# Low parts on another engine, an earlier normalisation and spread token parts in an attention kernel with two gated layers

## Chip, cores and metric

The kernel runs on one core of one Trainium2 chip. The time is the device time of one execution in microseconds, given as the median of three runs. Profile numbers come from one profiled execution, in us from its first instruction.

## What is computed

Pooled attention, then a gated layer, then a layer with a rational function, all in float32.

```python
k_p = k.reshape(B, H, Sp, pool, D).mean(axis=3)      # B, H = 8, 8; pool = 8; Sp = 72; D = 64
v_p = v.reshape(B, H, Sp, pool, D).mean(axis=3)
scores = scale * np.matmul(q, k_p.transpose(0, 1, 3, 2))
attn = softmax(scores)                               # maximum subtracted, sum + 1e-9
x = np.matmul(attn, v_p)                             # as 4608 tokens x 512
x = (silu(x @ w_gate) * (x @ w_val)) @ w_out         # 512 -> 1536 -> 512
h = x @ w_in                                         # 512 -> 2048
P = a[0] + a[1]*h + a[2]*h**2 + a[3]*h**3
Q = 1 + abs(b[0])*abs(h) + abs(b[1])*h**2
out = (P / (Q + 1e-6)) @ w_out2
```

## The kernel before

The 4608 tokens are nine blocks of 512. Every operand of a large product is held as two parts, a high one that TensorE takes at its fast float32 rate and a low one, the rest (`split`: ScalarE copies the high part, another engine subtracts). A product is then three matmuls per piece, high by high, low weights by high, high by low (`mm3`): the low part of the moving operand is wanted only in the last third.

The program writes the order of every engine by hand: each engine, and each queue of transfers (SP's, ScalarE's), carries out its instructions in the order of the program. `plan` holds the attention's steps by slot (one slot is one pass of f) and place; `place(stage, f, p)` runs what is due. The places of a pass are, in order, 0, A, B, B2 and C.

*Attention* works on units of up to 128 tokens. `scores` issues the score products; its four closures are `soft1` (VectorE: maximum per head, subtraction), `soft_exp` (ScalarE), `soft2` (VectorE: sum, 1e-9, reciprocal; then the product of probabilities and reciprocal, on GpSimd where `early` or `helped`) and `soft3` (copies `pr`). `transposes` turns the result on TensorE into PSUM banks of the pool that also holds the scores. In `attention_slots` a unit's `soft1` stands at place 0 of the slot after its scores, its exponential at A, its `soft2` at B2, and its `soft3` and transposes at 0 and A of the next slot.

*Start and block 0.* The first block's four units run by themselves (L509 to L578), with steps of `first` between them. `first` (class `Weights`) brings the first layer's weights from 64-bit words to float32 and into two parts, in a pipeline of four: ScalarE prepares the words (`words`), VectorE bounds, shifts and selects (L120, L121, L114) and GpSimd adds (L117), ScalarE copies the high part (L165), and `step` subtracts the low part (L149) on VectorE or on the engine that it is given. Block 0's loop (L754 on, j = 0) makes three steps in each of its 12 passes of f, two of them with GpSimd for the low part. A pass has three products: gate (`gp`), value (`vp`) and, one pass late, output (`acc`). L783 multiplies the silu by the value product, L788 makes its low part.

*Blocks 1 and 2* run the same loop, with sums of the weights (`weight_sums`) for what follows.

*The pairs' stage* (L878 to L952) takes six blocks as three pairs by a scheme of seven products for eight: 36 passes n, 12 for each pair. In a pass TensorE's chain is s1 (`cc`), s2 (`ca`), then the closing a22 of the pass before, a12 (`cb`), s4 (`cc`), the opening a11 of the next pass (`ca`, and ScalarE copies it to `cb`), and s3 (`ca`). Each uses its own part of the pair's tokens: t1, t2, t4, b21, b22, b11, t3. `token_part` splits one of them: two copies by ScalarE, two subtractions by VectorE (L94). Between the products VectorE sums banks: L901 after s2 (its result is the bank that s4 goes on with) and L937 after s3 (which must have read the bank before a22 goes on). While pair p runs, the next pair's attention runs in the same passes, the second layer's weights are converted (`second`: L120, L121, L114 by VectorE, L117 and the low part L94 by GpSimd), and in passes 2 to 9 the output weights' sums: `out_sums` (VectorE L651, then GpSimd L655 to L658) in one pass, `out_parts` (ScalarE, VectorE L94) in the next. Weights are streamed from memory two passes ahead (`stream`).

After it come the pairs' output products and the second layer, which the change leaves alone.

Of the kernel before, what the change touches and what calls it, by code (L numbers as in the profile page):

```python
# [13 lines left out]
AF = mybir.ActivationFunctionType  # L14
# [49 lines left out]
def attention_gated_rational(  # L64
# [277 lines left out]
    def scores(u, qt, early=False, helped=False):  # L342
# [25 lines left out]
        def soft1():  # L368
            for half in range(2):
                sc = banks[half]  # L370
                nc.vector.tensor_reduce(mx[:n, half], sc[:n], axis=AX.X, op=ALU.max)
                nc.vector.tensor_tensor(
                    pt[:n, half::2], sc[:n],
                    mx[:n, half].unsqueeze(2).to_broadcast([n, 4, SP]), op=ALU.subtract,
                )

        def soft_exp():
            nc.scalar.activation(pt[:n], pt[:n], AF.Exp, scale=1.0 / (POOL * math.sqrt(D)))

        def soft2():  # L380
            nc.vector.tensor_reduce(sm[:n], pt[:n], axis=AX.X, op=ALU.add)
            nc.vector.tensor_scalar(sm[:n], sm[:n], 1e-9, None, op0=ALU.add)
            nc.vector.reciprocal(sm[:n], sm[:n])
            (nc.gpsimd if early or helped else nc.vector).tensor_tensor(  # L384
                pt[:n], pt[:n], sm[:n].unsqueeze(2).to_broadcast([n, H, SP]), op=ALU.mult
            )

        def soft3():
            pairs = pt.rearrange("p (a i) s -> p a (i s)", i=2)
            for c in range(2):  # L390
                src = pairs[:n, 2 * c : 2 * c + 2, P:].unsqueeze(1).to_broadcast([n, 3, 2, REST])
                if early:
                    nc.scalar.activation(pr[:n, c], src, AF.Copy)
                else:
                    nc.gpsimd.tensor_copy(pr[:n, c], src)
# [69 lines left out]
    def attention_slots(js, start, helped=False):  # L465
# [16 lines left out]
        for n, (g, i) in enumerate(fl):  # L482
# [3 lines left out]
            put(slot, "C", lambda u=u: box.__setitem__(("s", u), scores(u, box.pop(("q", u)), helped=helped)))  # L486
            put(slot + 1, "0", lambda u=u: box["s", u][0]())
            put(slot + 1, "A", lambda u=u: box["s", u][1]())
            put(slot + 1, "B2", lambda u=u: box["s", u][2]())
# [24 lines left out]
    qts = {flat0[0]: qload(flat0[0], True, nc.scalar)}  # L514
    nc.scalar.dma_start(ident, ident_in)
# [3 lines left out]
    for u in flat0[1:]:  # L519
        qts[u] = qload(u, True, nc.scalar)  # L520
# [17 lines left out]
    soft = [scores(u, qts[u], True) for u in flat0]  # L538
# [14 lines left out]
    for n in range(2):  # L553
        soft[n][0]()
        soft[n][1]()
# [11 lines left out]
    for n in range(last):  # L567
        if n + 1 < last:
            turn(n + 1)
        for fn in evacs[n]:  # L570
            fn()
        if n:
            lows[n - 1]()
        lows[n] = values([flat0[n]], ptTs[n], None, x)
        if n + 1 < last:
            first.step(6)
# [165 lines left out]
    for j in range(PLAIN):  # L742
# [11 lines left out]
        for f in range(NF1):  # L754
# [20 lines left out]
            if j == 0:  # L775
                first.step(6, nc.gpsimd)
# [9 lines left out]
            if j == 0:  # L786
                first.step(6, nc.gpsimd)
# [92 lines left out]
    for key in ("t2", "b21", "b22", "t3", "t4"):  # L880
        token_part(0, key)
    stream(1)
    for n in range(full_n):
# [17 lines left out]
        nc.vector.tensor_tensor(c, cq[n][:, 0, :], bank_a[n], op=ALU.add)  # L901
        place(stage, f, "A")
        if n:
            end_chain(n - 1)
        if f == 0 and p:
            token_part(p, "t4")
# [9 lines left out]
        if more:  # L916
            token_part(p + 1, "b21")
# [4 lines left out]
        if more:  # L922
            token_part(p + 1, "b22")
# [13 lines left out]
        nc.vector.tensor_tensor(cq[n][:, 1, :], cq[n][:, 0, :], bank_a[n], op=ALU.add)  # L937
        if more:
            token_part(p + 1, "t3")
# [279 lines left out]
```

## Time and profile before

| | |
|---|---|
| Time, median of 3 runs | 1858.56 us (1857.02 to 1859.35) |
| Profiled execution, whole | 1855.71 us |
| Its span | 1853.9 us |
| TensorE busy | 1773.1 us, 96% of the span |
| VectorE busy | 1404.3 us, 76% |
| ScalarE busy | 1133.9 us, 61% |
| GpSimd busy | 365.4 us, 20% |

Engines: PE is TensorE, DVE VectorE, ACT ScalarE, POOL GpSimd. A matmul's record counts pipelined time, so a busy PE isn't PE at its peak; its idle time is real. The shares of the span are means over stages with different limits: block 0 runs from 41 to 168 us, blocks 1 and 2 to 425, the pairs' stage to about 870 (its third pair, without attention, from about 750 on), the rest after it. Spans on POOL are rough.

### The profile page before, as it was taken

The page shows a single profiled execution, that of the slowest core. Times are in us where ns is not written, and L with a number is a line of the kernel's source. Part 1 is how long each engine was busy: PE and PEld are TensorE (multiplying, and loading weights), DVE is VectorE, ACT ScalarE, POOL GpSimd, SP SyncE. Part 2 cuts the span into 40 slices and gives each one's busy share as a digit, 9 for nine tenths or more (in the row PEclk, how much of TensorE's full clock was granted, in tenths as well). Part 3 has the DMA queues.
Part 4 walks back from the last instruction along what each step waited for, and adds up shares of the span by engine and source line. Part 5 has one row for each costly group of instructions (what it writes and reads, how often), then busy time and mean ns, then how long its engine had stood idle before and what let it go on. Part 6 is the DMA issues. An engine that isn't in the chain of part 4 may idle for free.

```text
span 1853.9 us, 23836 instructions
## 1 busy us (share of the span) xinstructions
PE 1773.1 (96%) x8212; PEld 1428.0 (77%) x8212; DVE 1404.3 (76%) x2315; ACT 1133.9 (61%) x1972; POOL 365.4 (20%) x506
## 2 busy tenths in 40 slices
PE   5889999998999999999999999999999999999998
PEld 5667877776777777787888788888888888888887
DVE  8997665547667665644777798888888989888987
ACT  5676455546665664434455667676677677667665
POOL 2665555442344335221000000000000000000000
PEclk9999999999999999999999999999999999999999
DMA  7531757559999987999935801010101010101000
GB/s 257 192 109 48 237 166 237 193 185 320 326 336 309 309 313 260 301 341 380 337 148 193 284 1 46 1 46 1 46 1 46 1 46 1 46 1 46 1 24 23
DMA packets 157464, 285.27 MB, mean 154 GB/s; under 512 B 12320, under 2 KB 78496, under 8 KB 156320
## 3 DMA queue, kind: packets, MB, share of 16 engines
q1 hardware_dynamic: 156192, 282.64, 44.1%
q8 instruction: 65, 1.06, 0.2%
q10 hardware_dynamic: 1152, 1.12, 0.2%
q14 instruction: 55, 0.45, 0.1%
HBM read 194.58 MB, written 89.13 MB: 153 GB/s over the span
## 4 chain that ended last, share of the span: by engine, by line
PE 77%; DVE 11%; POOL 4%; ACT 3%; issue 3%; DMA 2%; SPq 0%; POOLq 0%; DVEq 0%; ACTq 0%
PE acco L256 21%; PE h L256 21%; PE ca L256 7%; PE ya L1062 5%; PE vp L256 4%; PE cc L256 3%; PE acc L256 3%; PE gp L256 3%; PE yc L1062 3%; PE cb L256 2%; PE pv L440 1%; PE yb L1062 1%; POOL p L384 1%; PE sc L363 1%; DVE tg L121 1%
## 5 line engine op out<-in xcount | busy, mean ns | idle before, releaser
L256 PE MATMUL acco<-wo,gt 128*128 128x512 f32 x1728 | 426.5, 395 | 2.7 <-ACT gt L1149 2.2
L256 PE MATMUL h<-z,wi 128*128 128x512 f32 x1728 | 422.4, 393 | 0.0
L256 PEld LDWEIGHTS acco<-wo,gt 128*128 128x128 f32 x1728 | 324.9, 188 | 80.9 <-ACT gt L1149 3.1
L256 PEld LDWEIGHTS h<-z,wi 128*128 128x128 f32 x1728 | 324.3, 188 | 75.6
L1128 ACT ACTIVATE sq<-h 128x512 f32<-128x512 f32 x144 | 86.4, 600 | 221.2 <-PE h L256 221.2
L1135 DVE SCALAR_TENSOR_TENSOR w<-sq,neg,w 128x512 f32<-128x512 f32 x144 | 108.0, 750 | 67.4 <-ACT w L1129 62.7
L256 PE MATMUL gp<-x,wg 128*128 128x512 f32 x432 | 109.6, 400 | 9.1 <-POOL wg L149 9.1
L1145 DVE SCALAR_TENSOR_TENSOR g<-t,neg,e 128x512 f32<-128x512 f32 x144 | 108.2, 751 | 5.1
L1132 ACT ACTIVATE t<-h,neg 128x512 f32<-128x512 f32 x144 | 111.8, 777 | 0.0
L1141 DVE SCALAR_TENSOR_TENSOR t<-t,neg,h 128x512 f32<-128x512 f32 x144 | 107.7, 748 | 5.1
L256 PE MATMUL vp<-x,wv 128*128 128x512 f32 x432 | 110.6, 403 | 0.4
L1142 DVE SCALAR_TENSOR_TENSOR e<-w,ln 128x512 f32<-128x512 f32 x144 | 98.7, 686 | 13.5 <-ACT ln L1139 13.4
L1139 ACT ACTIVATE ln<-ln,lnb 128x512 f32<-128x512 f32 x144 | 104.2, 724 | 4.7
L256 PE MATMUL acc<-ht,wo 128*128 128x512 f32 x432 | 106.5, 396 | 0.0
L1143 DVE SCALAR_TENSOR_TENSOR e<-e,ln 128x512 f32<-128x512 f32 x144 | 99.7, 692 | 5.0
L256 PEld LDWEIGHTS gp<-x,wg 128*128 128x128 f32 x432 | 79.4, 188 | 29.9 <-POOL wg L149 11.7
L1149 ACT ACTIVATE gt<-g 128x512 fp32r<-128x512 f32 x144 | 90.7, 630 | 16.9 <-DVE g L1145 16.9
L1129 ACT ACTIVATE w<-h,cab 128x512 f32<-128x512 f32 x144 | 98.5, 684 | 2.6 <-DVE e L1142 2.6
L1150 DVE TENSOR_TENSOR gt<-g,gt 128x512 fp32r<-128x512 f32 x144 | 98.6, 685 | 1.5 <-ACT gt L1149 0.8
L1140 DVE TENSOR_TENSOR t<-t,h 128x512 f32<-128x512 f32 x144 | 98.0, 680 | 0.0
L256 PEld LDWEIGHTS vp<-x,wv 128*128 128x128 f32 x432 | 80.7, 191 | 20.3 <-POOL wv L149 2.6
L256 PEld LDWEIGHTS acc<-ht,wo 128*128 128x128 f32 x432 | 80.4, 188 | 18.2
(246 smaller groups left out, 3186.4 us busy)
## 6 DMA issues: line engine op xcount, KB each, us to landing
sw<-sd SPq DMA_DIRECT2D x72, 512.0 KB, 7.2
sw<-wd SPq DMA_DIRECT2D x36, 512.0 KB, 5.8
h<-hq SPq DMA_DIRECT2D x36, 512.0 KB, 5.9
sd<-sp SPq DMA_DIRECT2D x24, 512.0 KB, 4.0
sw<-vd SPq DMA_DIRECT2D x36, 256.0 KB, 7.5
hl<-h SPq DMA_DIRECT2D x18, 512.0 KB, 7.2
hr<-h SPq DMA_DIRECT2D x18, 512.0 KB, 9.7
out<-ob SPq DMA_DIRECT2D x36, 256.0 KB, 4.1
```

Source lines behind the costliest of these rows:

```text
L256: nc.tensor.matmul(acc, st[:, lw, cols], mv[:, rw, mcols], start=first and i == 0, stop=last and i == n - 1, skip_group_check=seeded,)
L1062: nc.tensor.matmul(banks[q], w[:, lw, cols], t[:, rw, :], start=opened and k == 0 and m == 0, stop=k == NK - 1 and m == 2, skip_group_chec ...
L1129: nc.scalar.activation(w0, hps, AF.Abs, scale=cab[:, 4:5])
L1132: nc.scalar.activation(t, hps, AF.Identity, scale=neg[:, 3:4], bias=neg[:, 2:3])
L1135: nc.vector.scalar_tensor_tensor(w0, sq, neg[:, 5:6], w0, op0=ALU.mult, op1=ALU.add)
L1139: nc.scalar.activation(ln, ln, AF.Exp, scale=-1.0, bias=lnb)
L1140: nc.vector.tensor_tensor(t, t, hps, op=ALU.mult)
L1141: nc.vector.scalar_tensor_tensor(t, t, neg[:, 1:2], hps, op0=ALU.add, op1=ALU.mult)
L1142: nc.vector.scalar_tensor_tensor(e, w0, C1, ln, op0=ALU.add, op1=ALU.mult)
L1143: nc.vector.scalar_tensor_tensor(e, e, 2.0, ln, op0=ALU.subtract, op1=ALU.mult)
L1145: nc.vector.scalar_tensor_tensor(g, t, neg[:, 0:1], e, op0=ALU.add, op1=ALU.mult)
L1150: lambda gt=gt, g=g: nc.vector.tensor_tensor(gt[:, 1, :], g, f32(gt[:, 0, :]), op=ALU.subtract),
```

## The change

Six edits.

1. In block 0, the low parts that GpSimd made (`first.step(6, nc.gpsimd)`, two in a pass) are made by VectorE. The addition at L117 stays on GpSimd.
2. At the start, units 0 and 1 take a new form of the softmax (`heads`): no subtraction; VectorE scales the negative maximum, and ScalarE runs eight Exp per unit straight from the banks, each with the maximum as bias and its sum as accumulator. Both units' `soft1` and exponentials stand ahead of the v reductions.
3. q of unit 1 is loaded by SP's queue ahead of v, q of units 2 and 3 by SP's queue behind v, where all three went by ScalarE's.
4. The copies `pr` of block 0 are made by GpSimd, no longer by ScalarE, and one step of `first` (at n = 0 of the four turns) is left out, so that every later step comes one place later.
5. For the pairs' attention `soft2` stands at B, not B2; these slots begin in block 2.
6. Token parts: pair 0 splits only `t1` and `t2` ahead of its first pass; `b21` and `b22` follow L901 of that pass, `t3` the silu of `cc`, `t4` L937. For the later pairs `b11`, `t1`, `t2` stay in the last pass of the pair before, `b21` moves behind its L937, and `b22`, `t3`, `t4` into the first pass of their own pair.

```diff
-    def scores(u, qt, early=False, helped=False):
+    SCALE = 1.0 / (POOL * math.sqrt(D))
+    def scores(u, qt, early=False, helped=False, heads=False):
...
                 nc.vector.tensor_reduce(mx[:n, half], sc[:n], axis=AX.X, op=ALU.max)
+                if heads:
+                    continue
...
+            if heads:
+                nc.vector.tensor_scalar(mx[:n], mx[:n], -SCALE, None, op0=ALU.mult)
...
         def soft_exp():
-            nc.scalar.activation(pt[:n], pt[:n], AF.Exp, scale=1.0 / (POOL * math.sqrt(D)))
+            if not heads:
+                nc.scalar.activation(pt[:n], pt[:n], AF.Exp, scale=SCALE)
+                return
+            for half in range(2):
+                for c in range(NPAIR):
+                    h = 2 * c + half
+                    nc.scalar.activation(
+                        pt[:n, h], banks[half][:n, c], AF.Exp, scale=SCALE, bias=mx[:n, half, c : c + 1],
+                        accum_out=sm[:n, h : h + 1],
+                    )
...
-            nc.vector.tensor_reduce(sm[:n], pt[:n], axis=AX.X, op=ALU.add)
+            if not heads:
+                nc.vector.tensor_reduce(sm[:n], pt[:n], axis=AX.X, op=ALU.add)
...
-                if early:
-                    nc.scalar.activation(pr[:n, c], src, AF.Copy)
-                else:
-                    nc.gpsimd.tensor_copy(pr[:n, c], src)
+                nc.gpsimd.tensor_copy(pr[:n, c], src)
...
-            put(slot + 1, "B2", lambda u=u: box["s", u][2]())
+            put(slot + 1, "B" if js[0] >= PLAIN else "B2", lambda u=u: box["s", u][2]())
...
+    qts[flat0[1]] = qload(flat0[1], True)
...
-    for u in flat0[1:]:
-        qts[u] = qload(u, True, nc.scalar)
+    for u in flat0[2:]:
+        qts[u] = qload(u, True)
...
-    soft = [scores(u, qts[u], True) for u in flat0]
+    soft = [scores(u, qts[u], True, heads=n < 2) for n, u in enumerate(flat0)]
+    for n in range(2):
+        soft[n][0]()
+        soft[n][1]()
     for r in vruns:
         r()
...
-    for n in range(2):
-        soft[n][0]()
-        soft[n][1]()
...
-        if n + 1 < last:
+        if 0 < n < last - 1:
             first.step(6)
...
             if j == 0:
-                first.step(6, nc.gpsimd)
+                first.step(6)
...
     begin_chain(0)
-    for key in ("t2", "b21", "b22", "t3", "t4"):
-        token_part(0, key)
+    token_part(0, "t2")
...
         nc.vector.tensor_tensor(c, cq[n][:, 0, :], bank_a[n], op=ALU.add)
+        if f == 0:
+            if n == 0:
+                token_part(p, "b21")
+            token_part(p, "b22")
         place(stage, f, "A")
         if n:
             end_chain(n - 1)
-        if f == 0 and p:
-            token_part(p, "t4")
...
-        if more:
-            token_part(p + 1, "b21")
         run()
...
         nc.scalar.activation(hq[n][:, 1, :], c, AF.Silu)
-        if more:
-            token_part(p + 1, "b22")
+        if f == 0:
+            token_part(p, "t3")
...
         nc.vector.tensor_tensor(cq[n][:, 1, :], cq[n][:, 0, :], bank_a[n], op=ALU.add)
+        if f == 0:
+            token_part(p, "t4")
         if more:
-            token_part(p + 1, "t3")
+            token_part(p + 1, "b21")
```

## Rows read from the trace of the kernel before

**Rows 1.** Busy us (x instructions) by engine, PEclk, DMA share, GB/s, by stretch.
```profile
41.00:168.00 127.00, 109.16 (x521) 82.94 (x519) 122.38 (x182) 90.41 (x146) 79.45 (x69) 0.97 0.35 119
...
425.00:755.00 330.00, 301.84 (x1553) 241.71 (x1554) 220.43 (x433) 204.37 (x376) 125.22 (x175) 0.97 0.90 309
```
**Rows 2.** TensorE's waits, 425 to 755 us: total us, times, longest.
```profile
PE t L412 <- POOL p L384: 12.9, 8, 3.3
PE cc L256 <- DVE cc L901: 6.3, 3, 5.1
PE ca L256 <- DVE cq L937: 5.1, 2, 2.9
PE t L412 <- POOL pr L395: 2.5, 4, 0.6
PE t L416 <- DVE p L372: 1.3, 4, 0.4
```
**Rows 3.** Pieces in time at the start, VectorE: start, us, line, out<-in.
```profile
14.21 0.46 DVE L372 TENSOR_TENSOR p<-sc,mx 128x288 f32<-128x288 f32 x1
```
**Rows 4.** Groups by line, VectorE, 41 to 168 us: busy us, mean ns | idle.
```profile
L114 DVE SCALAR_TENSOR_TENSOR rawo<-rawo,to 128x512 uint32<-128x512 uint32 x11 | 14.5, 1316 | 0.4
L121 DVE TENSOR_SCALAR tg<-tg 128x512 uint32<-128x512 uint32 x10 | 13.9, 1392 | 0.3
L121 DVE TENSOR_SCALAR to<-to 128x512 uint32<-128x512 uint32 x11 | 13.7, 1247 | 0.4
...
L149 DVE TENSOR_TENSOR wo<-rawo,wo 128x512 fp32r<-128x512 f32 x9 | 6.2, 689 | 0.0
...
L121 DVE TENSOR_SCALAR tv<-tv 128x512 uint32<-128x512 uint32 x11 | 4.7, 427 | 0.4
```
**Rows 5.** Pieces in time in block 0, GpSimd and VectorE.
```profile
78.45 1.04 POOL L117 TENSOR_TENSOR rawo<-rawo 128x512 uint32<-128x512 uint32 x1 [0.63 <-DVE rawo L114]
79.45 1.51 POOL L149 TENSOR_TENSOR wv<-rawv,wv 128x512 fp32r<-128x512 f32 x1
...
78.89 0.89 DVE L120 TENSOR_SCALAR tg<-tg 128x512 f32<-128x512 f32 x1
79.81 1.43 DVE L121 TENSOR_SCALAR tg<-tg 128x512 uint32<-128x512 uint32 x1
```
**Rows 6.** Groups by line, GpSimd, 41 to 168 us.
```profile
L149 POOL TENSOR_TENSOR wg<-rawg,wg 128x512 fp32r<-128x512 f32 x9 | 13.4, 1485 | 0.0
```
**Rows 7.** Pieces at 460 us: ScalarE's exponential, VectorE's sum.
```profile
463.40 0.69 ACT L378 ACTIVATE p<-p 64x576 f32<-64x576 f32 x1
...
464.80 0.74 DVE L381 TENSOR_REDUCE sm<-p 64x8 f32<-64x576 f32 x1
```
**Rows 8.** Pieces at 488 us, GpSimd and TensorE.
```profile
488.22 0.72 POOL L658 TENSOR_TENSOR os<-or,os 128x256 f32<-128x256 f32 x1
488.90 1.15 POOL L384 TENSOR_TENSOR p<-p,sm 128x576 f32<-128x576 f32 x1
...
490.10 0.66 PE L412 MATMUL t<-ident,p 128*128 128x128 f32 x4 [3.30 <-POOL p L384]
```
**Rows 9.** Two short stretches, columns as in rows 1.
```profile
490.00:500.00 10.00, 9.90 (x48) 7.95 (x48) 3.82 (x8) 7.15 (x10) 1.86 (x5) 0.83 0.97 333
...
646.00:656.00 10.00, 10.00 (x44) 8.40 (x45) 2.50 (x6) 6.41 (x11) 3.34 (x6) 0.83 0.98 344
```
**Rows 10.** TensorE's waits, 300 to 425 us (block 2).
```profile
PE t L412 <- POOL p L384: 1.3, 1, 1.3
```
**Rows 11.** Pieces where pairs 0 and 1 begin, VectorE and TensorE.
```profile
434.31 2.49 DVE L94 TENSOR_TENSOR x0t<-t,x0t 128x512 fp32r<-128x512 f32 x4
...
443.86 1.52 PE L256 MATMUL ca<-x0t,sw 128*128 128x512 f32 x6
...
603.70 0.74 DVE L381 TENSOR_REDUCE sm<-p 128x8 f32<-128x576 f32 x1
...
602.91 1.52 PE L256 MATMUL ca<-x1t,sw 128*128 128x512 f32 x6
```

More of the change, by code (lines that the diff above doesn't have):

```diff
@@ L463, in attention_gated_rational, with attention_slots @@
     plan = {}
-    def attention_slots(js, start, helped=False):
+    def attention_slots(js, start, helped=False, heads=False):
         def put(slot, place, fn):
@@ L485, in attention_slots @@
             put(slot - 1, "B2", lambda u=u: box.__setitem__(("q", u), qload(u)))
-            put(slot, "C", lambda u=u: box.__setitem__(("s", u), scores(u, box.pop(("q", u)), helped=helped)))
+            put(slot, "C", lambda u=u: box.__setitem__(("s", u), scores(u, box.pop(("q", u)), False, helped, heads)))
             put(slot + 1, "0", lambda u=u: box["s", u][0]())
-            put(slot + 1, "A", lambda u=u: box["s", u][1]())
-            put(slot + 1, "B2", lambda u=u: box["s", u][2]())
+            put(slot + 1, "0" if heads else "A", lambda u=u: box["s", u][1]())
+            put(slot + 1, "B" if js[0] >= PLAIN else "B2", lambda u=u: box["s", u][2]())
             put(slot + 2, "0", lambda u=u: box.pop(("s", u))[3]())
@@ L786, in attention_gated_rational @@
             if j == 0:
-                first.step(6, nc.gpsimd)
+                first.step(6)
             nc.vector.tensor_tensor(ht[:, 1, :], hh, f32(ht[:, 0, :]), op=ALU.subtract)
```

## The prediction, made before the changed kernel was run

> **What bounds the kernel now.** I read the busy times by stage first [rows 1]. In block 0 (41 to 168 us) VectorE is busy for 122.4 of 127 us and TensorE for 109.2: VectorE sets the pace there. In the pairs' stage (425 to 755 us) VectorE is busy for only 220 of 330 us, and TensorE leaves 28 us empty, so single waits set the end. Before 41 us TensorE waits for the first units' softmax, on which VectorE works from 14 us on [rows 3]. Next I read what TensorE waits for in the pairs' stage [rows 2]: 12.9 us in eight waits for GpSimd's normalisation (`p`, L384), 2.5 us for its copies (`pr`), 1.3 us for VectorE to free a score bank (`p`, L372), 6.3 us for the sum at L901 (5.1 of it once), 5.1 us for the sum at L937 in two waits. Last I read durations in block 0 [rows 4] and the two engines beside each other [rows 5].
>
> **Low parts of block 0 by VectorE.** Twenty-two subtractions leave GpSimd, where one takes 1.49 us [rows 6]. On VectorE the same line takes 0.69 us, with 0.6 from start to start [rows 4]: plus 13.2 us on the engine that sets the pace. Against it stands blocked time. The same tensor_scalar takes 0.43 us on one tile and 1.39 on another, and the selection on `rawo` takes 1.32 us where that on `rawv` takes 0.69 [rows 4]. The pieces show why: VectorE's 0.43 us operation begun at 79.81 ends only after GpSimd's low part that began at 79.45, and the operation at 78.89 lasts until after GpSimd's addition that began at 78.45 [rows 5]. Three groups alone lose 10 x 0.96 + 11 x 0.82 + 11 x 0.63 = 25.6 us. About 1.98 us per pass of f stand beside a low part, 21.8 us in eleven passes, and that part goes. The additions at L117 (1.04 us, three per pass) stay, and now find the moved low parts, which read two tiles, right behind them. I lay a pass out by starts: selection of `g`, low part first, the addition waits, then blocks the next operation for 0.9 us; the second addition runs beside the product with a bank (0.6 us not blocked) and holds the next low part for 0.5; the third lies behind the reductions. That is 1.4 us per pass where about 0.95 stand now (0.47 at 78.89 [rows 5], the rest on `to`). Sum: 13.2 - 21.8 + 11 x 0.45 = -3.6, and I take **-4.0** since GpSimd also starts its additions sooner. Bounds: -12 if the three groups' loss goes whole, +14 if none goes.
>
> The Trainium skill speaks on both sides here. "SBUF — State Buffer", section Who interferes with whom, says that a VectorE instruction with two SBUF inputs, or in a two-port mode, and a GpSimd instruction that reads SBUF exclude each other for a whole instruction, and the pieces agree: 1.43 us instead of 0.43 [rows 5]. By it alone, with every remaining addition blocking VectorE for its full 1.04 us, 33 x 1.04 in place of 11 x 0.95, this term would be about 13.2 - 21.8 + 23.9 = +15.3, near rival (1).
>
> **The start.** For units 0 and 1 four subtractions of 0.46 us go [rows 3] and two sums of 0.74 us [rows 7]; two scalings of about 0.2 come; one step of the weights (a bound, a shift and a selection, 1.5 us, and a low part of 0.6) moves to the end of the block. On VectorE this is -1.84 - 1.48 + 0.4 - 2.1 = -5.0. The maxima move ahead of the v reductions into time in which VectorE waits for loads (+1.6 back), but the missing step also covered TensorE's first values, so VectorE then waits some 1.8 us for them: **-4.8**. Sixteen short Exp with an accumulator take the place of two, and none is in this trace: at the most each takes as long as the whole one, 0.69 us [rows 7], 11 us together, of which about 3 would show; at the least they show nowhere. ScalarE is idle there, so I take none; bounds for the start -7 and +1. The q loads change from ScalarE's queue to SP's, unit 1's ahead of v, the others behind it; v then lands by one load later at most, which I count in the 1.8. The copies `pr` by GpSimd in place of ScalarE I take at nothing: GpSimd waits there for the reciprocals. The displaced step returns at f = 10 and 11, where the last steps were empty: **+1.3** (bounds 0 and 2.1).
>
> **Normalisation at B instead of B2.** Around 488 us the chain is plain: GpSimd ends its four sums of the output weights (the last at 488.22), only then runs `p` at 488.90 for 1.15 us, and TensorE's transposes start at 490.10 after 3.30 us of idling [rows 8]. At B the same work stands in front of those sums, of GpSimd's low parts and, on VectorE, of the additions at L651. By program order three more products and the next unit's scores (about 5 us) then lie between, so 12.9 + 2.5 should go. What is late next is the score bank: the transposes use banks that the next unit's subtraction frees, and behind the low part of the output weights VectorE is still busy with it; I leave 2 us of such waits. **-13.4**. The granted clock is 0.83 over 490 to 500 us [rows 9], 1.7 us lost to the lower of its two levels (1.2 GHz) after the 3.3 us gap, and it is 0.83 again over 646 to 656 us, behind another of the eight waits: **-3.4** for the two. In block 2, where the same line changes, one such wait of 1.3 us stands [rows 10], with 0.5 of bank waits: **-1.8**; there the product of the gate comes 1.1 us later behind the sum, and the output product that needs it runs a whole pass later, which covers it. Bounds for these three together: -8 and -21.
>
> VectorE now meets the sum at B, so what stands behind it waits if the exponential isn't done: the output weights' additions, then L937 and, through it, the last product of the chain. In a pass at 460 us the exponential ends at 464.09 and VectorE asks for it at 464.80 [rows 7], so I count nothing.
>
> **Token parts between the products.** They issue nothing on SP's queue; on ScalarE their high halves now stand ahead of one exponential per pair, and pair 0's second stream is asked for ahead of them. In pair 0 eight of the ten halves leave VectorE's queue in front of L901, where four of them take 2.49 us [rows 11]. By the new order: scores' maxima and subtractions to 433.7, L901 to 434.3, `b21` to 435.5, `b22` to 436.7, the conversion and the softmax sum to 438.8; ScalarE's silu tables and both silu hold `t3`'s high half until 440, so its low half ends at 440.9 and the product s3 at 441.3. It ended at 443.86 + 1.52 = 445.4 [rows 11]: **-4.1** (bounds -5 and -2). In pair 1 VectorE's queue is full (no idle time stands ahead of the sum at 603.70). `t3` now stands behind all of it but `t4`: it ends where the sum at 603.70 began, less `t4`'s 1.2 us, plus 1.0 for the sum and its reciprocal, at 603.5; s3 then ends at 604.0 instead of 604.4 [rows 11]. The wait at L937 goes and a new one before s3 comes: **0** (bounds -2 and +2). Pair 2 has no attention: its wait of 2.9 us at L937 [rows 2] and the fallen clock behind it (1.7) go, as VectorE then reaches `t3` just when s3 wants it: **-4.6** (bounds -5 and -2).
>
> Sum: -4.0 - 4.8 + 1.3 - 13.4 - 3.4 - 1.8 - 4.1 - 4.6 = **-34.8**. The profiled execution took 1855.7 us, so 1820.9; the median of the runs lies 2.9 us above it, so **1823.7**.
>
> **The rivals.** (1) Block 0 pays the whole price: the low parts cost 13.2 us and the additions take over the blocking. For it speaks VectorE's 96%; against it that most of the blocked time stands beside a low part. 1823.7 + 4.0 + 13.2 = 1841. The skill's "Perfetto Trace Analysis", section Optimizing Scalar/DVE Operations, points this way: with VectorE saturated, move work off it, to GpSimd even; but it adds that the shared port may leave nothing gained. (2) A second pacemaker lies just behind the gaps of the pairs' stage: the DMA engines are at 0.90 there [rows 1], and score banks and ScalarE's table loads follow. If half of the stage's 25.5 us stays, 1836; with all of it, 1849. (3) The other side: the sum at B catches VectorE in front of an unfinished exponential. Place: each of 18 units of the pairs' stage. Today the margin is 0.7 us [rows 7]; behind L937 lie two products and the next scores, about 4 us, before its bank is wanted, so this decides only if the exponentials come over 4 us later than now. Then the normalisation's 16.8 us are lost and each further us costs 18: from 2 us further on it is 1823.7 + 16.8 + 36 = 1876. Against it: the exponential's own inputs move forward too. (4) Block 0 gives back nearly all blocked time: 1814.
>
> **How the numbers follow.** Forecast 0.60, its own range 1815 to 1831; (1) 0.16; (2) 0.13; (3) 0.04; (4) 0.07. The range 1809 to 1841 takes in (4), (1) and the better half of (2). A difference of 0.2%, 3.7 us, is about what a measurement here can tell from none; faster by more than that: 0.93, within it 0.03, slower 0.04.
>
> **What would show it.** Right: in block 0 GpSimd has no L149 left, VectorE's L121 groups fall from 1.25 to 1.4 us towards 0.6 to 0.8, and a pass of block 0 is 0.3 to 0.5 us shorter; the first product of block 0 starts some 5 us sooner; no wait of TensorE for `p` above 0.5 us after 425 us; L901 and L937 no longer among its releasers, a wait before s3 of some 3 us in pair 1 instead. Wrong: L117 beside long tensor_scalars in every pass, a pairs' stage as long as before with waits for loads, or VectorE idle in front of the sum at B.

## The result, and the profile after

| | before | after |
|---|---|---|
| Time, median of 4 runs | 1857.79 us (1856.61 to 1859.35) | 1836.53 us (1836.46 to 1837.38) |
| Ratio | | 0.9884 (95% interval 0.9872 to 0.9897) |
| Profiled execution, its span | 1855.71, 1853.9 us | 1836.46, 1834.7 us |
| First product of block 0 | 39.99 us | 39.67 us |

The change saved 21.3 us where 34.8 were forecast. To see where, I laid the two traces side by side at one instruction that every pass has, ScalarE's silu (L773, now L791, in the blocks; L921, now L934, in the pairs' stage). How much sooner it starts after the change, from one place to the next, is what each stage gained, in us:

| Stretch | Forecast | Measured |
|---|---|---|
| Start, to the first silu | -4.8 | -0.5 |
| Block 0, passes 0 to 10 | -4.0 | -5.3 |
| Block 0, last pass (the displaced step) | +1.3 | +2.0 |
| Blocks 1 and 2 | -1.8 | +0.1 |
| Pair 0, first pass | -4.1 | -3.3 |
| Pair 0, other passes | -16.8 with the next but one | -5.5 |
| Pair 1, first pass | 0 | +2.1 |
| Pair 1, other passes | (see above) | -5.6 |
| Pair 2, first pass | -4.6 | -3.7 |
| The rest | 0 | +0.7 |
| Sum | -34.8 | -19.2 (spans: 1834.7 - 1853.9; the rounded lines give -19.0) |

The medians of four runs each differ by 21.3 us, the two profiled executions by 19.2.

Busy us by engine (instructions), PEclk, DMA share and GB/s, the same two stretches as in [rows 1]:

```profile
41.00:168.00 127.00, 112.19 (x534) 85.30 (x533) 120.26 (x207) 92.78 (x151) 55.18 (x57) 0.98 0.36 123
...
425.00:755.00 330.00, 317.59 (x1622) 252.77 (x1620) 229.60 (x447) 208.56 (x387) 132.46 (x181) 0.98 0.92 327
```

TensorE's waits in the pairs' stage after the change, 425 to 755 us (us in total, times, the longest), to be set beside [rows 2]:

```profile
PE t L433 <- POOL pr L412: 5.6, 4, 2.5
PE ca L256 <- DVE x1t L94: 2.1, 2, 1.1
PE cc L256 <- DVE cc L918: 1.2, 2, 0.6
PE ca L256 <- DMA sw<-wd: 0.9, 1, 0.9
```

The eight waits for `p` (12.9 us) are gone, and of L901 (now L918) and L937 (now L954) 1.2 us are left. In their place stand four waits for the copies `pr`, 5.6 us where there were 2.5, and two in front of s3, for low parts of `t3`. In pieces, GpSimd and TensorE at 480 us, the pass that answers to [rows 8]:

```profile
476.56 1.48 POOL L404 TENSOR_TENSOR p<-p,sm 128x576 f32<-128x576 f32 x1
478.01 1.44 POOL L94 TENSOR_TENSOR rawi<-rawi 128x256 fp32r<-128x256 f32 x2
479.41 0.71 POOL L673 TENSOR_TENSOR os<-or 128x256 f32<-128x256 f32 x1
...
481.57 0.72 POOL L676 TENSOR_TENSOR os<-or,os 128x256 f32<-128x256 f32 x1
482.23 0.47 POOL L412 COPY pr<-p 128x96 f32<-128x96 f32 x2
...
479.45 0.60 PE L429 MATMUL t<-ident,p 128*128 128x128 f32 x4
482.55 0.52 PE L433 MATMUL t<-ident,pr 128*96 128x128 f32 x2 [2.50 <-POOL pr L412]
```

The product `p` ends at 478.04 and TensorE transposes it at 479.45 without a wait. But the transposes have a second half that reads `pr`, and the two copies that make it, 0.47 us long, still stand at place 0 of the next slot: behind the low parts and the four sums that `p` has just been moved ahead of. TensorE waits 2.50 us, where it waited 3.30. ("PSUM — Partial Sum Buffer" of the Trainium skill, section Engine vs sequencer instructions, says that GpSimd's queue is strictly first in, first out; this agrees: copies that could run at 478.04 run at 482.23.)

Block 0 went as laid out. VectorE's groups, 41 to 168 us (busy us, mean ns), the lines of [rows 4] among them:

```profile
L149 DVE TENSOR_TENSOR wg<-rawg,wg 128x512 fp32r<-128x512 f32 x9 | 10.8, 1202 | 0.0
L120 DVE TENSOR_SCALAR tv<-tv 128x512 f32<-128x512 f32 x11 | 10.5, 956 | 0.0
...
L114 DVE SCALAR_TENSOR_TENSOR rawo<-rawo,to 128x512 uint32<-128x512 uint32 x11 | 7.6, 694 | 0.4
...
L121 DVE TENSOR_SCALAR to<-to 128x512 uint32<-128x512 uint32 x11 | 5.0, 454 | 0.4
L121 DVE TENSOR_SCALAR tg<-tg 128x512 uint32<-128x512 uint32 x11 | 4.7, 427 | 0.4
```

The three groups that lost 25.6 us are back at 0.43 to 0.69 us each. What is blocked now are two operations in each pass, and the pieces show both (answering [rows 5]):

```profile
73.16 1.37 POOL L117 TENSOR_TENSOR rawg<-rawg 128x512 uint32<-128x512 uint32 x1 [2.28 <-DVE rawg L114]
76.13 1.04 POOL L117 TENSOR_TENSOR rawv<-rawv 128x512 uint32<-128x512 uint32 x1 [1.60 <-DVE rawv L114]
...
72.94 0.68 DVE L149 TENSOR_TENSOR wo<-rawo,wo 128x512 fp32r<-128x512 f32 x1
73.54 1.26 DVE L120 TENSOR_SCALAR tv<-tv 128x512 f32<-128x512 f32 x1
...
75.91 0.68 DVE L801 TENSOR_TENSOR hh<-hh,vp 128x512 f32<-128x512 f32 x1
76.51 1.21 DVE L149 TENSOR_TENSOR wg<-rawg,wg 128x512 fp32r<-128x512 f32 x1
```

L120 takes 1.26 us in place of 0.42 (it ends just behind GpSimd's addition, at 74.80 against 74.53), and the low part 1.21 in place of 0.69: 0.84 + 0.52 = 1.4 us per pass, as the prediction laid it out (0.9 + 0.5). The product with a bank at 75.91 runs beside the addition at its usual 0.68 us, also as laid out. The first addition takes 1.37 us itself where the second of the pass takes 1.04: it started beside a low part that reads two tiles, so the blocking goes both ways. "SBUF — State Buffer" of the Trainium skill, section Who interferes with whom, says which operations take part (two SBUF inputs or a two-port mode against a GpSimd instruction that reads SBUF) and that whoever came first holds the other off; the pieces agree, down to the product with a bank that is spared. The full price that the prediction worked out from that page (+15.3 us) took each of the 33 additions as blocking for its whole length. It didn't come: the third addition of the pass shown (79.38 us) lies beside reductions of `v`, which take their usual 0.68 us, and the second spends its first 0.5 us beside the product with a bank.

In block 2 the wait for `p` of [rows 10] became a wait for a score bank (TensorE's waits, 297 to 425 us; before, the same line was 1.0 us in two waits):

```profile
PE t L429 <- DVE p L379: 1.4, 2, 1.0
```

And the start: GpSimd, VectorE and TensorE from 16 to 29 us, start and us of each piece.

```profile
23.23 1.15 POOL L404 TENSOR_TENSOR p<-p,sm 128x576 f32<-128x576 f32 x1 [1.28 <-DVE sm L403]
25.53 1.04 POOL L117 TENSOR_TENSOR rawg<-rawg 128x512 uint32<-128x512 uint32 x1 [1.15 <-ACT pt L437]
26.97 1.15 POOL L404 TENSOR_TENSOR p<-p,sm 128x576 f32<-128x576 f32 x1 [0.41 <-DVE sm L403]
28.06 0.89 POOL L412 COPY p<-p 128x96 f32<-128x96 f32 x4
...
18.19 0.46 DVE L376 TENSOR_REDUCE mx<-sc 128x4 f32<-128x288 f32 x1 [1.59 <-PE sc L368]
...
16.17 3.69 PE L368 MATMUL sc<-kr,q 64*128 64x72 f32 x32 [5.54 <-DMA q<-in_q]
...
28.38 0.66 PE L433 MATMUL t<-ident,p 128*96 128x128 f32 x2 [5.07 <-POOL p L412]
```

The same thing once more: unit 1's copies, moved from ScalarE to GpSimd, are ready to run when unit 1's product ends at 21.54 us, but in GpSimd's order they stand behind the products of units 2 and 3 and an addition of the weights, and run at 28.06. TensorE idles 5.07 us for them. The other two pieces show a second loss, ahead of the softmax sums of units 2 and 3: TensorE waits 5.54 us for q of unit 2, which edit 3 put behind v in SP's queue, and VectorE stands idle for 1.59 us until these scores are there.

### The profile page after: what moved, and what is told of

Its sections match the earlier page's. It is cut to its first block, busy times and chain, and to the rows that moved or that the text cites. A ratio compares the mean times of both kernels' runs of the same rounds, so it can differ in the third digit from the quotient of the medians.

```text
span 1834.7 us, 23841 instructions
## 1 busy us (share of the span) xinstructions
PE 1772.9 (97%) x8212; PEld 1425.9 (78%) x8212; DVE 1403.0 (76%) x2333; ACT 1135.3 (62%) x1994; POOL 342.8 (19%) x492
## 4 chain that ended last, share of the span: by engine, by line
PE 61%; DMA 1%; DVE 1%; ACT 0%; issue 0%; POOL 0%; SPq 0%; DVEq 0%; ACTq 0%
PE acco L256 22%; PE h L256 21%; PE ya L1081 5%; PE ca L256 4%; PE yc L1081 3%; PE cc L256 2%; PE yb L1081 1%; PE cb L256 1%; DMA sw<-wd 0%; DMA hl<-h 0%; PE pv L457 0%; DMA os<-so 0%; POOL t L722 0%; PE sc L368 0%; DVE gt L1169 0%
## 5 line engine op out<-in xcount | busy, mean ns | idle before, releaser
L1161 DVE SCALAR_TENSOR_TENSOR e<-w,ln 128x512 f32<-128x512 f32 x144 | 98.7, 686 | 13.5 <-ACT ln L1158 13.4
L1168 ACT ACTIVATE gt<-g 128x512 fp32r<-128x512 f32 x144 | 91.0, 632 | 16.8 <-DVE g L1164 16.8
```

The source lines that it names most:

```text
L1161: nc.vector.scalar_tensor_tensor(e, w0, C1, ln, op0=ALU.add, op1=ALU.mult)
```

## Experiments

Each kernel is the changed kernel with one edit more, unless it says otherwise. All were run beside the kernel before. The ratio is the record's own and not the quotient of the two medians. An interval of a ratio is about 0.15% to either side, 3 us, so a term smaller than that is read from the traces, aligned at the start of its stage.

| Kernel | Median us | Ratio to before (95%) | Less than before, us |
|---|---|---|---|
| a0 changed, once more | 1835.75 | 0.9881 (0.9865 to 0.9897) | 21.9 |
| e1 pr at B | 1825.33 | 0.9821 (0.9806 to 0.9836) | 31.9 |
| e2 pr by ScalarE at the start | 1835.86 | 0.9874 (0.9858 to 0.9890) | 21.4 |
| e3 low parts by GpSimd | 1842.01 | 0.9917 (0.9895 to 0.9939) | 15.2 |
| e4 t3 sooner | 1830.56 | 0.9850 (0.9835 to 0.9864) | 26.7 |
| e5 normalisation at B2 | 1843.60 | 0.9923 (0.9908 to 0.9938) | 14.1 |
| e6 step kept | 1832.86 | 0.9870 (0.9855 to 0.9884) | 24.8 |
| e7 token parts as before | 1839.34 | 0.9898 (0.9884 to 0.9913) | 18.4 |
| e8 start as before | 1834.24 | 0.9873 (0.9856 to 0.9889) | 23.5 |
| e9 three mendings | 1821.20 | 0.9799 (0.9784 to 0.9813) | 36.5 |
| e10 block 0 at B too | 1820.36 | 0.9805 (0.9791 to 0.9820) | 37.3 |
| e11 three mendings, step kept | 1818.28 | 0.9794 (0.9778 to 0.9811) | 39.3 |

### e1: the copies at B too

```diff
-            put(slot + 2, "0", lambda u=u: box.pop(("s", u))[3]())
+            if js[0] >= PLAIN:
+                put(slot + 1, "B", lambda u=u: box["s", u][3]())
+            else:
+                put(slot + 2, "0", lambda u=u: box.pop(("s", u))[3]())
```

> The changed kernel, with the copies pr (L412) of the pairs' attention at B, right behind the product of probabilities and reciprocal, and no longer at 0 of the next slot. Theory: what is left of the expected gain of the earlier normalisation is lost because GpSimd meets these copies behind the four sums of the output weights (L673 to L676). Then TensorE's four waits for pr between 480 and 636 us go (2.5 + 0.6 + 0.5 + 2.0 = 5.6 us) and with them the two stretches of fallen clock behind the long ones (483 and 637 us, 1.7 us each): 9.0 us less than the changed kernel, about 1827.5. Rival: the stage is held by something else as well (loads at 0.92, score banks), and half or more of this stays: 1832 or above.

It took 1825.33 us, 11.2 less than the changed kernel. The first lines of TensorE's waits, 425 to 755 us, hold no `pr` any more:

```profile
PE ca L256 <- DVE x1t L94: 2.1, 2, 1.1
PE cc L256 <- DVE cc L921: 1.2, 2, 0.6
PE ca L256 <- DMA sw<-wd: 0.8, 1, 0.8
```

Its start happened to be 1.4 us earlier; within the pairs' stage the silu gains 10.8 us on the changed kernel, 4.5 around 480 us (2.5 of wait, the rest mostly the clock, which fell to 0.83 over 480 to 490 us in the one and stayed at 1.00 in the other), 2.1 from there to 541, 3.7 around 630 and 0.6 behind it. So the missing gain of the normalisation lay in two copies of 0.26 us, and no load and no bank stepped in (the longest wait for a load is 0.8 us): the rival fell.

### e2: the copies of the start by ScalarE

```diff
-                nc.gpsimd.tensor_copy(pr[:n, c], src)
+                if early:
+                    nc.scalar.activation(pr[:n, c], src, AF.Copy)
+                else:
+                    nc.gpsimd.tensor_copy(pr[:n, c], src)
```

> The changed kernel, with the copies pr of the first block's units by ScalarE, as in the kernel before. Theory: at the start GpSimd meets unit 1's copies behind the products of units 2 and 3 and an addition of the weights, and TensorE's transposes of unit 1 start at 28.38 us instead of some 24; VectorE has unit 0's evacuated part ready at 27.3, so the products with v start there and not at 28.84, and the first product of block 0 at about 38.2 instead of 39.67: 1.5 us less. Rival: the start is set by the loads and by VectorE's work, and nothing changes (within 0.4 us).

1835.86 us: by time alone no difference that can be told. In the trace unit 1's transposes of `pr` start at 23.34 us and no longer at 28.38. The starts of these kernels differ by themselves (a0, below), so I measured from VectorE's sum of unit 3, the last of the softmax sums, to the first product: 13.1 us here, 14.4 in six profiles with the changed start (a0's is 14.8), 13.5 in both profiles with the old one. The copies on GpSimd cost 1.3 us; the theory had 1.5.

### e3: the low parts back on GpSimd

```diff
             if j == 0:
-                first.step(6)
+                first.step(6, nc.gpsimd)
             steps[1]()
...
             if j == 0:
-                first.step(6)
+                first.step(6, nc.gpsimd)
```

> The changed kernel, with two of the three low parts of each pass of block 0 by GpSimd again. Theory: the 0.4 to 0.7 us by which each of the first eleven passes became shorter come from these low parts, and all of them go back: 5.3 us more, about 1842, with VectorE's selections at 1.25 to 1.4 us again. Rival: the passes became shorter through the other edits at the start (the steps that come one place later): less than 2 us more.

1842.01 us, 5.5 more. Pass by pass the silu falls back by 0.4 to 0.8 us, 5.5 in ten passes and 6.3 with the last, and the blocked groups are back, now on other tiles because the steps come one place later: L121 on `to` at 1.38 us, the selection on `rawv` at 1.33. The low parts carry all of the gain of block 0's passes.

### e4: t3 ahead of the exponential

```diff
             token_part(p, "b22")
+            if p:
+                token_part(p, "t3")
         place(stage, f, "A")
...
-        if f == 0:
+        if f == 0 and p == 0:
             token_part(p, "t3")
```

> The changed kernel, with t3 of the second and third pair split ahead of the exponential of their first pass (behind b22) and not behind the silu of the same pass. Theory: in the second pair's first pass ScalarE's exponential and its two table loads (3.3 us, 582.8 to 586.1) stand ahead of t3's high halves, so the product s3 waits 2.4 us in three pieces, and the clock falls behind it (1.7 us): 4.1 us less, about 1832.5, all of it between 584 and 602 us. Rival: the exponential then comes 2.5 us later and VectorE's sum at B waits for it, or the silu's bank comes free too late: within 1 us of the changed kernel.

What stands around `t3` in the changed kernel's pieces of that pass (ScalarE, VectorE, GpSimd, TensorE):

```profile
582.77 1.28 ACT L389 ACT_TABLE_LOAD   x1
584.06 0.69 ACT L389 ACTIVATE p<-p 128x576 f32<-128x576 f32 x1
584.77 1.28 ACT L934 ACT_TABLE_LOAD   x1
...
587.03 1.15 ACT L93 ACTIVATE x1t<-t 128x512 fp32r<-128x512 f32 x2
...
588.44 0.74 DVE L401 TENSOR_REDUCE sm<-p 128x8 f32<-128x576 f32 x1
...
589.54 2.20 DVE L94 TENSOR_TENSOR x1t<-t,x1t 128x512 fp32r<-128x512 f32 x2
...
589.77 1.42 POOL L404 TENSOR_TENSOR p<-p,sm 128x576 f32<-128x576 f32 x1 [1.69 <-DVE sm L403]
...
587.72 1.48 PE L256 MATMUL ca<-x1t,sw 128*128 128x512 f32 x4 [0.27 <-ACT x1t L93]
590.24 0.50 PE L256 MATMUL ca<-x1t,sw 128*128 128x512 f32 x1 [1.04 <-DVE x1t L94]
591.79 0.50 PE L256 MATMUL ca<-x1t,sw 128*128 128x512 f32 x1 [1.05 <-DVE x1t L94]
```

ScalarE spends 582.77 to 586.05 on the exponential and its two tables, and does `t3`'s two high halves from 587.03 to 588.18 (the next pair of high halves in its queue, to 590.03, is `t4`'s). For them TensorE waits only 0.27 us. Its 2.1 us of waits for the low halves come from VectorE and GpSimd: VectorE's softmax sum and reciprocal (588.44 to 589.62), which edit 5 put there, stand ahead of the two low parts, and these then take 2.20 us, where `b22`'s two, at 583.85, take 1.29, since they lie beside the normalisation's product. The expectation's reason, the exponential ahead of the high halves, is therefore not what e4 shows: it moves `t3` as a whole, out of reach of the sum and the product too, and in e5, where ScalarE keeps the exponential there, the waits for the low halves are gone as well.

The run took 1830.56 us, 6.0 less. By the trace this pass gained 2.4 us and not 4.1: the low halves now stand in front of L860, for which TensorE waits 1.30 us, and a wait of 0.81 for a score bank follows. In pair 2 the same edit costs 0.5 us.

```profile
585.61 1.66 PE L256 MATMUL ca<-x1b,sw 128*128 128x512 f32 x6 [1.30 <-DVE hq L860]
...
593.43 0.63 PE L429 MATMUL t<-ident,p 128*128 128x128 f32 x4 [0.81 <-DVE p L379]
```

Another 1.6 us is no work of the edit: behind the wait of 1.99 us for `pr` near 634 us, which both kernels have, the clock fell in one and not in the other. Granted clock is the third number from the end (changed kernel, then this one; the wait ends at 636.12 in the one and at 632.33 in the other):

```profile
634.00:644.00 10.00, 8.01 (x35) 6.56 (x33) 4.06 (x10) 5.37 (x8) 4.04 (x8) 0.83 0.93 327
```

```profile
632.00:642.00 10.00, 9.67 (x52) 8.01 (x54) 3.50 (x9) 7.71 (x13) 5.05 (x9) 1.00 0.98 353
```

### e5: the normalisation at B2 again

```diff
-            put(slot + 1, "B" if js[0] >= PLAIN else "B2", lambda u=u: box["s", u][2]())
+            put(slot + 1, "B2", lambda u=u: box["s", u][2]())
```

> The changed kernel, with the pairs' normalisation at B2 again (edit 5 undone, all else kept). Theory: in the pairs' stage outside the first passes of its pairs the traces of before and after differ by 5.5 and 5.7 us, and this is edit 5 alone, though the copies pr held back a part of it: 11.2 us more, about 1847.7, with TensorE's waits for p (L404) back in the stage; in block 2 within 0.3 us, since there the wait only changed its releaser. Rival: those passes became shorter through the token parts: under 6 us more.

```profile
PE t L429 <- POOL p L404: 12.8, 8, 3.3
PE t L429 <- POOL pr L412: 2.5, 4, 0.6
```

1843.60 us, 7.1 more (7.9 against a0). The waits of [rows 2] are back, to a tenth of a us. By stages: other passes of pair 0 5.5 us longer, of pair 1 5.7 longer, blocks 1 and 2 unchanged, as expected; but the first pass of pair 1 became 3.0 us shorter, which the expectation left out: `t3`'s low parts stand ahead of the sum again and take their 1.28 us, and the two waits in front of s3 aren't there.

```profile
592.96 1.28 DVE L94 TENSOR_TENSOR x1t<-t,x1t 128x512 fp32r<-128x512 f32 x2
594.16 0.74 DVE L401 TENSOR_REDUCE sm<-p 128x8 f32<-128x576 f32 x1
```

### e7: the token parts as before

```diff
-    token_part(0, "t2")
+    for key in ("t2", "b21", "b22", "t3", "t4"):
+        token_part(0, key)
...
-        if f == 0:
-            token_part(p, "t3")
+        if more:
+            token_part(p + 1, "b22")
...
```

> The changed kernel, with the token parts in their old order (edit 6 undone). Theory, from the two traces: the first pass of pair 0 3.3 us longer with its 5 us wait at L918 (the old L901) back, that of pair 1 2.1 us shorter, since t3 comes a pass sooner again and s3 does not wait for it, that of pair 2 3.7 us longer with a wait at L954 (the old L937): 4.9 us more in all, about 1841.4. Rival: the loss in pair 1 comes from the normalisation at B, which now stands in the same queue: then pair 1 gets no shorter, and the sum is 7 us more.

```profile
PE cc L256 <- DVE cc L919: 6.8, 4, 5.1
PE t L433 <- POOL pr L412: 5.5, 4, 2.5
PE ca L256 <- DVE cq L955: 5.1, 2, 2.9
```

1839.34 us, 2.8 more (3.6 against a0). The first passes: pair 0 4.4 us longer, pair 1 2.8 shorter, pair 2 4.8 longer. Between them 1.5 us came back because the clock didn't fall near 483 us this time (granted clock 1.00 over 480 to 490 us, 0.83 in the changed kernel), behind the same 2.49 us of wait. So the token parts save 9.2 us in two pairs and lose 2.8 in the third, and the loss is there only when edits 5 and 6 are both made, since undoing either takes it away (e5, e7). The rival of a loss that stays fell.

### a0, e6, e8: the start

a0 is the changed kernel as it is. e6 has the step back:

```diff
-        if 0 < n < last - 1:
+        if n + 1 < last:
             first.step(6)
```

> The changed kernel once more, unchanged, as a measure of how much its start differs from one execution to another. In its first profile the first product of block 0 started at 39.67 us; in six profiles of kernels with the same start it was 37.8 to 38.7 (mean of these with it 38.6). Theory: the start differs by itself, with the landing of the first loads: 37.8 to 39.7 here, and the time 1834.5 to 1837. Rival: 39.7 within 0.2 us, so that the others came sooner for a reason of their own.

> The changed kernel with the left-out step of the weights back at n = 0 of the four turns. Theory: the last pass of block 0 loses the 2.0 us that the step brought there; at the start VectorE's 2.1 us for it fall mostly into the 2.2 us in which VectorE waits behind unit 0's low part for the late copies pr (27.3 to 29.5 us), so the first product comes 0.5 us later at the most: 1.5 us less in all. Rival, the prediction's reading: the step costs its whole 2.1 us ahead of the first product, and the sum is zero.

e8 undoes edits 2 to 4:

```diff
-    soft = [scores(u, qts[u], True, heads=n < 2) for n, u in enumerate(flat0)]
-    for n in range(2):
-        soft[n][0]()
-        soft[n][1]()
+    soft = [scores(u, qts[u], True) for n, u in enumerate(flat0)]
     for r in vruns:
         r()
...
-        if 0 < n < last - 1:
+        if n + 1 < last:
...
```

> The changed kernel, with the start as in the kernel before: softmax of units 0 and 1 by subtraction behind the v reductions, q by ScalarE's queue, pr by ScalarE, the step of the weights not left out (edits 2 to 4 undone). Theory: the new start moves the first product of block 0 forward by only some 1.4 us (mean of four profiles with it, 38.6, against 39.99), and the step that it moves to the end of the block costs 2.0 there: together within 1.5 us of the changed kernel, rather below it (about 1836). Rival, the prediction's terms (4.8 less 1.3): 3.5 us more, 1840.

| Profile | VectorE's sum of unit 3 starts | First product of block 0 | Between |
|---|---|---|---|
| before, e8 (old start) | 26.52, 27.00 | 39.99, 40.48 | 13.5 |
| after, a0, e1, e3, e4, e5, e7 (new start) | 23.5 to 25.3, mean 24.2 | 37.8 to 39.7, mean 38.6 | 14.4 (a0 14.8) |
| e6 (step kept) | 24.04 | 39.21 | 15.2 |
| e2, e9, e10 (pr by ScalarE) | 24.2 to 24.6 | 37.2 to 37.7 | 13.0 to 13.3 |
| e11 (pr by ScalarE, step kept) | 24.84 | 38.31 | 13.5 |

Times: a0 1835.75, e6 1832.86, e8 1834.24 us. a0 began its first product at 39.55, so the range of 37.8 to 39.7 is the start's own, and the first profile lay at its late end. The new start is 1.6 us earlier on the mean (40.2 to 38.6): 2.6 up to the last softmax sum, 0.9 given back behind it. In the last pass of block 0, e6 and e8 each gain 2.3 us on the changed kernel: the displaced step's price. Behind it they gain 0.9 more, since the clock doesn't fall there; but that part is not paid each time, for e2, with the step displaced, shows no fall there either. So edits 2 to 4 gain 1.6 and cost about as much or more, and undoing them all changes nothing that the time can tell (1.5 us less than a0). No run undoes edit 3 alone. Of the step alone, e6 tells: 0.8 us ahead of the first product, 2.3 to 3.1 at the end of the block, 2.9 in the medians, which is no more than the interval.

### e9, e10, e11: mended

e9 joins e1 and e2, and splits `t3` of the second and third pair in two: high halves ahead of the exponential, low halves behind L861.

```diff
...
+            if p:
+                src, tiles = t3_high(p)
         place(stage, f, "A")
         if n:
             end_chain(n - 1)
+        if f == 0 and p:
+            for i in range(2):
+                nc.vector.tensor_tensor(tiles[i][:, 1, :], src[:, i, :], f32(tiles[i][:, 0, :]), op=ALU.subtract)
...
-        if f == 0:
+        if f == 0 and p == 0:
             token_part(p, "t3")
```

> The changed kernel with three mendings: pr of the pairs' attention at B, pr of the first block by ScalarE, and for the second and third pair t3's high halves ahead of the exponential, its low halves behind L861. Theory: the first is worth 10.8 us (trace of that run by itself, without the start's variation), the second 1.3 (from VectorE's sum of unit 3 to the first product of block 0, 13.1 us against 14.4), the third 4, of which a new wait of 1.3 us for L860 goes when the low halves follow L861: in all 16 less, about 1820. Rival: the loads (0.92) or score banks hold the stage by now, so that the gains do not add: 1824 or above.

1821.20 us. The gains add up to 14.6 of the 16 expected against a0; the pairs' stage, 425 to 755 us, now runs so:

```profile
425.00:755.00 330.00, 324.39 (x1687) 261.71 (x1686) 235.58 (x460) 212.89 (x397) 138.27 (x187) 1.00 0.96 341
```

TensorE works 324.4 of 330 us at the full granted clock, with the DMA engines at 0.96. Of the waits one of 1.5 us for a score bank is the longest, and one of 0.5 us is for a load. A second pacemaker at a DMA share of 0.90 there was not.

e10 moves block 1's normalisation in block 0 to B as well (`"B" if helped`).

> The kernel with the three mendings, with the normalisation and the copies pr at B in block 0 too (block 1's attention). Theory: TensorE's four waits for p in block 0 (5.8 us, the longest 2.2) go, but VectorE is busy for 95% of block 0, and the normalisation there only changes its place in VectorE's queue: 2 us less than with the three, about 1819. Rival A: the waits go whole, 5.8 us less, 1815.4. Rival B: VectorE meets the sum ahead of its work on the weights, and TensorE waits for low parts in place of p: no change.

1820.36 us, 0.8 less than e9, which can't be told from none. TensorE's waits in block 0, 41 to 170 us:

```profile
PE vp L256 <- DVE wv L149: 5.9, 6, 1.9
PE gp L256 <- DVE wg L149: 4.6, 8, 1.3
PE t L432 <- DVE p L379: 1.5, 1, 1.5
```

The waits for `p` (5.9 us in e9) are gone, those for low parts of `wg` have grown from 2.1 to 4.6 us and score banks come to 2.6: where VectorE sets the pace, an earlier place for one piece of its work is a later one for the next. Silu by silu block 0 is 3.0 us longer than in e9 to its last pass, and 3.9 us come back behind it, where e9's last wait for `p` (2.19 us at 162.85) and the fall of the clock behind it are gone. So rival B named the right mechanism, but its "no change" is the sum of two terms.

e11 is e9 with e6's line.

> The kernel with the three mendings, and the left-out step of the weights back at n = 0 as well. Theory: with the step kept the changed kernel took 2.9 us less, since the step cost 0.8 us ahead of the first product and saved 2.3 in the last pass and 0.9 behind it; if that adds to the three, 1818.3. Rival: the step was cheap only because VectorE waited 2.2 us for the late copies pr; with pr by ScalarE this wait is gone, the step costs its 2.1 us ahead of the first product (39.3 us instead of 37.2), and the time is within 1.2 us of the 1821.2 of the kernel with the three.

1818.28 us, 2.9 less than e9 by the medians, what e6 had given by itself; the ratios, 0.9794 and 0.9799, can't be told apart. In the trace the last pass gains 2.3 us and the stretch behind it 0.9, as in e6. The step cost 0.5 us between the last softmax sum and the first product (13.5 against 13.0), not its 2.1: the rival, that only the wait for the late copies hid it, fell. By the median this is the fastest of these kernels, 39.3 us below the kernel before.

## Why the prediction was right, and where it was not

The sign, the range (1809 to 1841) and most mechanisms held; the forecast's own range, 1815 to 1831, did not, and the gain was 21.3 us of 34.8. The range held by the room that it left for the rivals, not by the sum. Of the signs named, the durations in block 0 and the end of the waits for `p` came; the first product some 5 us sooner did not, nor did L901 leave the list of waits.

- **Low parts: right.** Forecast -4.0, measured -5.3 in ten passes, e3 by itself 5.5. The 1.4 us of remaining blocking per pass are there as laid out. Rival (1) and the page's full price would have shown passes longer than before.
- **The start: wrong in two terms**, -4.8 forecast and 1.6 us gained on the mean.
  - *The loads.* Up to the last softmax sum the working's terms give 1.84 + 1.48 - 0.4 + 1.6 = 4.5 us (its "+1.6 back" is a gain: only so do the terms give -4.8); 2.6 came. The rest lies at the loads. VectorE's last reduction of v ends at 13.81 and 14.29 us in the two profiles with the old start and at 15.0 to 16.3 in the seven with the new one, and VectorE then stands idle for 0.7 to 1.6 us until unit 2's scores are there, for which TensorE waits for q. The prediction saw v land one load later and counted that in 1.8 us of waiting; it left out that q of unit 2 lands behind v. That edit 3 does both is argued from its order, no run shows its share.
  - *The copies.* Wrong also was "The copies `pr` by GpSimd in place of ScalarE I take at nothing: GpSimd waits there for the reciprocals": they cost 1.3 us (e2). GpSimd waits for reciprocals indeed, but for those of units 2 and 3, in front of unit 1's copies.
  - *The left-out step*, 2.1 us less work and 1.8 of waiting in its place, is worth 0.3 by the working, 0.8 by e6 and 0.5 by e11: between the last sum and the first product VectorE waits 2.7 us for ScalarE in e9, without the step, and 0.4 in e11, with it. At the end of the block the step cost 2.0 to 2.3 in place of 1.3, at the edge of the bound given (2.1).
- **Normalisation: mechanism right, one step missing.** "so 12.9 + 2.5 should go": the 12.9 went; the 2.5, waits for `pr`, grew to 5.6. The prediction moved `soft2` past the output weights' sums and left out that `soft3` is not moved by edit 5, though its rows list the waits for `pr` beside those for `p` [rows 2]. With it moved (e1) the stage gives 10.8 us more, which with the 11.1 measured is more than the 16.8 forecast. The 2 us of bank waits didn't come; 16.6 of the 21.9 are waits that left the list, and where all of the other 5.3 lie (3.4 was put on the clock) isn't shown.
- **The clock.** Two falls, 3.4 us, were to go with their waits. Two of the long waits stayed, under another name, and the falls behind them too. e4 and e7 show that a wait of 2.0 or 2.5 us has a fall behind it in one execution and none in another, so 1.7 us is the price of a fall, and not of every long wait.
- **Block 2: wrong.** -1.8 forecast, nothing measured, and e5 confirms it: the transposes there need a bank that the next unit's subtraction frees (L379), and that stands behind the low part of `ht` and one of the weights' sums on VectorE. The prediction had seen 0.5 us of such waits and added its terms up; but a wait for two things is worth only what the earlier of the two leaves.
- **Token parts: right in pairs 0 and 2** (-4.1 and -4.6 forecast; 4.4 and 4.8 by e7).
- **Token parts: wrong in pair 1** (0 forecast, +2.1, bound +2). From the last silu of pair 0 to the end of s3 it is 17.13 us before and 17.68 after, where the working has 0.4 us less than before. The queue that I laid out for VectorE was right as far as its order goes, the sum included; left out was the product of edit 5 beside `t3`'s low halves (2.20 us in place of 1.29). Set on the time scale of the kernel before, they end at 604.4 us, where the working has 603.5. The other 1.5 us lie behind s3: the granted clock is 0.75 and 0.90 in the two halves of 590 to 600 us, behind the new waits, and the working set the new wait against the old one without a fall of its own. In e5 sum and product stand behind the low halves, the clock stays at 1.00, and the stretch to the end of s3 takes 15.67 us. Each edit was costed by itself, and this 3 us belongs to the pair of them.
- **Rivals.** (2) had the time, 1836, but not the reason: its second pacemaker was to be loads, score banks or table loads; the loads weren't (e9), the table loads weren't (0.27 us in pair 1), a score bank was in block 2, and most of the loss in the pairs' stage was GpSimd's own order. That its time was met is chance. (3) needed the sum to meet an unfinished exponential: in none of the stage's 18 units does it. In the tightest the exponential ends at 693.69 us and the sum starts at 694.39, the same 0.7 us as before the change.

## What to carry to other kernels

When a step is moved ahead in a queue, follow its result to the end of the chain: the next small instruction on the same engine that wasn't moved keeps the old place in the order, and the wait goes there (here two copies of 0.26 us held back 10.8 us). What an edit costs in the order of one queue depends on what the other edits put beside it in the neighbouring queues; cost the edits one by one, then walk through each stage once more with all of them in place. And a wait for two releasers is worth no more than the distance to the second.

## What the runs showed of the hardware that was not expected

- Sixteen short Exp with an accumulator, whose cost the prediction could only bound, start every 0.30 us (0.31 to 0.41 for each, and a read of its accumulator of 0.19 to 0.30 beside the next), 4.9 us in all, where the two whole ones before took 0.68 each.
- One and the same start differs by 2 us from one execution to another (first product 37.8 to 39.7 us in the seven profiles with it).
- Blocking is mutual: GpSimd's addition of 1.04 us took 1.37 where it began beside a VectorE operation that reads two tiles, and two low parts of `t3` took 2.20 us in place of 1.29 beside GpSimd's product.
- An equal wait of TensorE is followed by a fall of the granted clock towards its lower level (1.2 GHz) in one execution and by none in another (over 10 us, 0.83 and 1.00 behind 2.0 us near 634, and again around 2.5 us near 483).
